# Attention plus linear attention on one core: normalisation in pieces, a new start, two spare PSUM banks in the first chunk, a reordered tail

## Chip, cores, metric

One core of one Trainium2 chip. The metric is the device time of one execution in microseconds (us). Times are medians of several executions. The engines are TensorE (PE in the profile, PEld for its weight loads), VectorE (DVE), ScalarE (ACT), GpSimd (POOL) and SyncE (SP).

## The reference, cut to what matters

```python
# B, S, D = 1, 2048, 640; 32 heads of 20; all bf16
q, k, v = split_heads(x @ wqkv)                    # part A
p = softmax(einsum("bhqd,bhkd->bhqk", q, k) * 20 ** -0.5)
a = merge_heads(einsum("bhqk,bhkd->bhqd", p, v)) @ wo

pq, pk = phi(q), phi(k)                            # part B, its own x, wqkv, wo
num = einsum("bhqd,bhde->bhqe", pq, einsum("bhsd,bhse->bhde", pk, v))
b = merge_heads(num / (pq . sum(pk) + 1e-6)) @ wo  # linear attention
out = concatenate([a, b], axis=-1)
```

Part A needs 2048 x 2048 x 32 exponentials. They fix the time: everything else has to fit beside them.

## The kernel before

A *unit* is one head's scores for 128 keys and 512 queries, one PSUM bank. There are 2048 units. They are handled in groups of three: TensorE writes the scores of a group in three banks, ScalarE takes one exp over the three, TensorE multiplies the result with V ("PV"). Two sets of three banks alternate, one bank collects PV, and one *spare bank* serves all other matmuls: the Q, K and V projections, the output projection and all of part B. These run in the background, in steps that fill the spare bank and are copied out by VectorE. One *chunk* is 64 units: a group of 4 heads against 512 queries. At its end the PV result is normalised.

The main loop, in program order. In the timelines shown below, each engine works through its own instructions in this order:

```python
for j in range(NG):                     # NG groups
    if j + 1 < NG:
        self.emit_scores(j + 1)         # TensorE
    self.emit_exp(j)                    # ScalarE
    self.flush_later(j)                 # what self.at(dj, ...) put off to this group
    ...                                 # emit_pv, and norm(n) at the end of a chunk
    ...                                 # budget: 1600 columns while j < 30, later less
    self.bg(budget)                     # background steps into the spare bank
    self.ahead(min(j + 4, NG - 1))
    self.fill(1200 if j > 20 else 0)    # idle matmuls that keep TensorE busy
```

The normalisation: five VectorE instructions, straight one behind the other.

```python
sch.op("dve", lambda e: e.tensor_copy(self.OTr[:, sl], ps[:, b, sl]), ...)
sch.op("dve", lambda e: e.transpose(tr, self.OTr[:, sl]), ...)
sch.op("dve", lambda e: e.reciprocal(rt, tr[:, 0:w:32]), ...)
sch.op("dve", lambda e: e.transpose(tr, rt.unsqueeze(2).broadcast_to(...)), ...)
sch.op("dve", lambda e: e.tensor_tensor(self.OTn[:, os_, sl], tr, self.OTr[:, sl], op=ALU.mult), ...)
```

The end of a Q or K projection step, which frees the spare bank:

```python
sch.op("dve", lambda e: e.tensor_copy(dst, ps[:, b, :]), reads=(("ps", b),), writes=(res,))
sch.op("dve", lambda e: e.tensor_reduce(mx, dst, axis=AX.X, op=ALU.max, ...), ...)
```

The loads: SyncE issues the rows of x and then 15 transposed loads of x (three sets of five, one set for each further 512 tokens). At the same time ScalarE's queue brings three weight loads of 800 KB.

## Time and profile before

1056.07 us, median of 3 runs (1055.41 to 1056.4). The profiled execution took 1050.0 us with a span of 1048.2, so it is one of the quicker ones.

From the page: busy times; the chain that ended last, by engine and by line; and the two costliest groups of instructions (after "|" the busy time and the mean ns of one, then the engine's idle time before them and what ended it).

```profile
PE 791.8 (76%) x5849; PEld 256.7 (24%) x5905; DVE 381.4 (36%) x752; ACT 952.7 (91%) x743; POOL 26.9 (3%) x42
...
ACT 65%; PE 21%; DVE 11%; issue 1%; DMA 1%; SPq 0%; POOL 0%; POOLq 0%; DVEq 0%
...
L1045 ACT ACTIVATE f_PT<-ps 128x1536 bf16<-128x1536 f32 (+1 forms) x683 | 935.5, 1551 | 67.7 <-PE ps L153 67.0
L153 PE MATMUL ps<-f_Qr,f_KT 32*128 32x512 bf16 x2048 | 285.9, 413 | 159.8 <-ACT f_PT L1045 151.3
```

ScalarE is the bound. The exps fill 935.5 us, and when ScalarE waits for one, it waits for scores. The question is only when it idles. I cut the span in four: to the first exp; from there to the end of unit 72; from there to the end of the last exp; the tail. The windows view gives busy time by engine for the last three (columns: length, PE, PEld, DVE, ACT, POOL, granted clock, DMA share, GB/s). ScalarE's idle time is the length less its busy time. Where the timeline merges exps into one entry, the end of unit 72 is interpolated in it.

```profile
11.61:51.59 39.98, 32.88 (x255) 13.47 (x258) 17.27 (x31) 33.03 (x25) 22.57 (x31) 0.91 0.64 103
51.59:1033.58 981.99, 747.30 (x5525) 237.09 (x5576) 349.54 (x692) 915.59 (x712) 1.10 (x4) 0.90 0.05 14
1033.58:1048.20 14.62, 5.87 (x37) 2.92 (x35) 7.45 (x18) 1.59 (x4) 0.00 (x0) 0.81 0.14 49
```

So 6.9 us idle in the first part, 66.4 us in the middle, and a tail of 14.62 us. The middle is where the time is. The timeline around the end of the fourth chunk shows one of its stalls (columns: start, length, what; in brackets the idle time before it and what ended it):

```profile
146.84 0.69 DVE L1079 COPY f_OTr<-ps 128x512 f32<-128x512 f32 x1 [2.04 <-PE ps L153]
147.42 0.39 PE L153 MATMUL ps<-f_Qr,f_KT 32*128 32x512 bf16 x3 [0.63 <-ACT f_PT L1045]
147.57 0.71 DVE L1086 STREAM_TRANSPOSE f_Tr<-f_OTr 128x512 f32<-128x512 f32 x1
148.31 0.25 DVE L1087 RECIPROCAL f_Rt<-f_Tr 128x16 f32<-128x16 f32 x1
148.60 0.71 DVE L1088 STREAM_TRANSPOSE f_Tr<-f_Rt 128x512 f32<-128x512 f32 x1
149.35 0.69 DVE L1091 TENSOR_TENSOR f_OTn<-f_Tr,f_OTr 128x512 bf16<-128x512 f32 x1
149.96 0.68 DVE L983 CAST f_KT<-ps 128x512 bf16<-128x512 f32 x1
150.68 0.69 DVE L984 TENSOR_REDUCE f_kmx<-f_KT 128x1 f32<-128x512 bf16 x1
151.10 1.49 PE L153 MATMUL ps<-f_xT,f_arw 128*128 128x512 bf16 x3 [3.29 <-DVE f_KT L983]
152.52 0.61 PE L153 MATMUL ps<-f_Qr,f_KT 32*128 32x512 bf16 x3
...
153.18 1.45 ACT L1045 ACTIVATE f_PT<-ps 128x1536 bf16<-128x1536 f32 x1 [3.13 <-PE ps L153]
```

Read it from the bottom. The exp at 153.18 waited 3.13 us for scores. TensorE could not issue them, because ahead of them in its order stood a K projection that waited 3.29 us for the spare bank. The copy that frees the bank (the CAST at 149.96) stood behind the five instructions of the normalisation. The projection matmuls that follow take 1.49 us for three: TensorE had also lost half of its clock (0.50 granted from 150 to 158 us).

### The profile page before, as it was taken

The numbers are of one execution on the slowest core, as the hardware profiler recorded it, in microseconds if no ns is written. First come the engines' busy times: TensorE is split into PE (matmuls) and PEld (weight loads), VectorE is DVE, ScalarE is ACT, GpSimd is POOL, SyncE is SP. The second block draws the span as 40 slices with busy tenths as digits, with TensorE's granted clock in tenths as the row PEclk, the third lists the DMA queues.
The fourth block names the chain that finished last, engine by engine and source line by source line (L and its number), as shares of the span: only waits on it lengthen the run. The fifth ranks groups of instructions, "written<-read, shape, count | busy, mean of one in ns | idle before, by whom it ended". The sixth has DMA issues, their size and how long they took to land.

```text
span 1048.2 us, 13498 instructions
## 1 busy us (share of the span) xinstructions
PE 791.8 (76%) x5849; PEld 256.7 (24%) x5905; DVE 381.4 (36%) x752; ACT 952.7 (91%) x743; POOL 26.9 (3%) x42
## 2 busy tenths in 40 slices
PE   6888778877787786777777777877777877768775
PEld 3332322322222222222221212212212222112222
DVE  4544344434323334333222443244341243352123
ACT  4979889999899999999998989888999989998895
POOL 5400000000000000000000000000000000000000
PEclk8989989999889989899998878878999889997898
DMA  8400000050001010010001000100000000000000
GB/s 197 62 1 1 1 1 1 1 151 1 8 13 32 1 26 1 2 26 1 1 13 38 2 0 14 38 1 7 25 21 13 13 7 14 7 1 14 13 1 28
DMA packets 40410, 20.81 MB, mean 20 GB/s; under 512 B 31896, under 2 KB 39704, under 8 KB 40344
## 3 DMA queue, kind: packets, MB, share of 16 engines
q1 hardware_dynamic: 37064, 17.21, 7.0%
q10 hardware_dynamic: 3280, 2.66, 0.9%
q8 instruction: 48, 0.79, 0.3%
q14 instruction: 18, 0.15, 0.0%
HBM read 7.41 MB, written 5.24 MB: 12 GB/s over the span
## 4 chain that ended last, share of the span: by engine, by line
ACT 65%; PE 21%; DVE 11%; issue 1%; DMA 1%; SPq 0%; POOL 0%; POOLq 0%; DVEq 0%
ACT f_PT L1045 63%; PE ps L153 21%; DVE f_Tr L1088 2%; DVE f_Tr L1086 2%; DVE f_OTr L1079 2%; ACT f_ex L1207 2%; DVE f_OTn L1091 2%; DMA f_xT<-in_A_x_dram 1%; DVE f_KT L983 1%; DVE f_Rt L1087 1%; DVE f_r L1204 0%; SPq L889 0%; DVE f_pk L1345 0%; PE ps L1357 0%; DVE f_Qr L983 0%
## 5 line engine op out<-in xcount | busy, mean ns | idle before, releaser
L1045 ACT ACTIVATE f_PT<-ps 128x1536 bf16<-128x1536 f32 (+1 forms) x683 | 935.5, 1551 | 67.7 <-PE ps L153 67.0
L153 PE MATMUL ps<-f_Qr,f_KT 32*128 32x512 bf16 x2048 | 285.9, 413 | 159.8 <-ACT f_PT L1045 151.3
L153 PE MATMUL ps<-f_PT,f_V 128*21 128x512 bf16 x2048 | 217.1, 419 | 0.0
L153 PEld LDWEIGHTS ps<-f_Qr,f_KT 32*128 32x128 bf16 x2048 | 66.8, 92 | 385.1 <-ACT f_PT L1045 324.7
L153 PEld LDWEIGHTS ps<-f_PT,f_V 128*21 128x21 bf16 x2048 | 49.7, 89 | 130.1 <-issue 128.7
L153 PE MATMUL ps<-f_arw,f_arb 128*128 128x320 bf16 x320 | 66.4, 320 | 11.5 <-DVE f_r L1204 11.2
L153 PE MATMUL ps<-f_wo,f_OTn 128*128 128x320 bf16 x256 | 59.8, 339 | 14.7 <-DVE f_OTn L1091 6.0
L1204 DVE COPY f_r<-ps 128x320 f32<-128x320 f32 (+1 forms) x52 | 29.5, 566 | 92.6 <-PE ps L153 92.6
L983 DVE CAST f_Qr<-ps 128x512 bf16<-128x512 f32 x32 | 22.1, 690 | 86.5 <-PE ps L153 86.5
L153 PE MATMUL ps<-f_xT,f_arw 128*128 128x512 bf16 x144 | 43.8, 404 | 11.6 <-DVE f_KT L983 4.9
L153 PE MATMUL ps<-f_xT,f_wqp 128*128 128x512 bf16 x134 | 45.5, 411 | 5.4 <-issue 4.0
L153 PE MATMUL ps<-f_woB,f_pk 128*128 128x320 bf16 x160 | 37.7, 359 | 14.5 <-DVE f_st L1386 6.4
L1079 DVE COPY f_OTr<-ps 128x512 f32<-128x512 f32 (+1 forms) x33 | 22.2, 674 | 68.9 <-PE ps L153 68.8
L1210 DVE TENSOR_SCALAR f_ex<-f_ex 128x320 f32<-128x320 f32 (+1 forms) x52 | 18.9, 364 | 70.5 <-ACT f_ex L1207 70.5
L1173 DVE CAST f_st<-ps 128x320 bf16<-128x320 f32 x24 | 11.8, 490 | 83.6 <-PE ps L153 83.6
L1207 ACT ACTIVATE f_ex<-f_r 128x320 f32<-128x320 f32 (+1 forms) x52 | 32.3, 621 | 9.7 <-DVE f_r L1204 9.7
L983 DVE CAST f_KT<-ps 128x512 bf16<-128x512 f32 x32 | 22.1, 689 | 47.0 <-PE ps L153 47.0
L153 PE MATMUL ps<-f_arw,f_xT 128*128 128x160 bf16 x320 | 32.3, 250 | 8.8 <-DVE f_KT L983 7.5
L1386 DVE CAST f_st<-ps 128x320 bf16<-128x320 f32 x32 | 15.7, 490 | 60.4 <-PE ps L153 60.4
L153 PE MATMUL ps<-f_arb,f_arw 128*128 128x512 bf16 x90 | 32.2, 427 | 6.6 <-DVE f_r L1204 4.7
L153 PEld LDWEIGHTS ps<-f_arw,f_arb 128*128 128x128 bf16 x320 | 26.1, 101 | 45.2 <-issue 21.1
L153 PEld LDWEIGHTS ps<-f_wo,f_OTn 128*128 128x128 bf16 x256 | 19.9, 104 | 46.9 <-issue 21.0
(73 smaller groups left out, 426.4 us busy)
## 6 DMA issues: line engine op xcount, KB each, us to landing
out_dram<-f_st SPq DMA_DIRECT2D x32, 160.0 KB, 1.8
f_arw<-in_B_wqkv_dram SPq DMA_DIRECT2D x1, 2400.0 KB, 8.4
f_arb<-in_A_wqkv_dram ACTq DMA_DIRECT2D x2, 800.0 KB, 12.0
f_arw<-in_A_wqkv_dram ACTq DMA_DIRECT2D x1, 800.0 KB, 8.8
f_wo<-in_A_wo_dram SPq DMA_DIRECT2D x4, 200.0 KB
f_woB<-in_B_wo_dram SPq DMA_DIRECT2D x1, 800.0 KB, 10.1
f_st<-in_A_x_dram SPq DMA_DIRECT2D x2, 320.0 KB
f_arb<-in_B_x_dram SPq DMA_TRANSPOSE x40, 2.7
```

Of the source, the lines that this page charges most:

```text
L153: lambda e: e.matmul(out, lhsT, rhs, start=start, stop=stop, tile_position=tp, skip_group_check=sgc),
L983: sch.op("dve", lambda e: e.tensor_copy(dst, ps[:, b, :]), reads=(("ps", b),), writes=(res,))
L1045: sch.op("act", lambda e: e.activation(self.PT[:, s0:s0 + n, :], ps[:, b0:b0 + n, :], AF.Exp, scale=scale), reads=tuple(("ps", b0 + k) for ...
L1079: sch.op("dve", lambda e: e.tensor_copy(self.OTr[:, sl], ps[:, b, sl]), reads=(("ps", b),), writes=(("OTr", k),))
L1086: sch.op("dve", lambda e: e.transpose(tr, self.OTr[:, sl]), reads=res, writes=(("Tr", k),))
L1088: sch.op("dve", lambda e: e.transpose(tr, rt.unsqueeze(2).broadcast_to([128, w // 32, 32])), reads=(("Rt", k),), writes=(("Tr", k),))
L1091: sch.op("dve", lambda e: e.tensor_tensor(self.OTn[:, os_, sl], tr, self.OTr[:, sl], op=ALU.mult), reads=(("Tr", k),) + res, writes=wr)
L1173: sch.op("dve", lambda e: e.tensor_copy(dst, ps[:, b, 0:320]), reads=(("ps", b),), writes=(("stage", s, h),))
L1204: sch.op("dve", lambda e: e.tensor_copy(tt, ps[:, b, 0:n]), reads=(("ps", b),), writes=(("r1", k),))
L1207: sch.op("act", lambda e: e.activation(ex, tt, AF.Exp), reads=(("r1", k),), writes=(("ex", k),))
L1210: sch.op("dve", lambda e: e.tensor_scalar(ex, ex, 1.0, 1e-6, op0=ALU.min, op1=ALU.add), reads=(("ex", k),), writes=(("ex", k),))
L1386: sch.op("dve", lambda e: e.tensor_copy(dst, ps[:, b, 0:320]), reads=(("ps", b),), writes=(("stage", s, h),))
```

## The change

Its intent: (1) give the normalisation out in pieces over the next three groups, and put off the max-reductions, the mask steps and phi's exp; (2) start sooner: a warm-up of TensorE, the first Q and K tiles in pieces on two engines, and the weight loads after the first set of transposed loads, through GpSimd's queue; (3) in the first 72 units groups of 3, 2, 3, 2, 3, 2, 2, 1, which free a second spare bank; (4) output partials done before the last exp, and a tail without stores between the halves. The core of the diff:

```diff
-            sch.op("dve", lambda e: e.transpose(tr, self.OTr[:, sl]), ...)
-            sch.op("dve", lambda e: e.reciprocal(rt, tr[:, 0:w:32]), ...)
-            ...
+            def f1(...): ...      # transpose
+            def f2(...): ...      # reciprocal
+            def f3(...): ...      # transpose
+            def f4(...): ...      # multiply, then norm_done(n)
             if last:
-                self.tail_out(range(4 * qc + 2 * k, 4 * qc + 2 * k + 2))
+                for f in (f1, f2, f3, f4):
+                    f()
+            else:
+                for d, f in ((1, f1), (2, f2), (2, f3), (3, f4)):
+                    self.at(d, f)
+        if last:
+            self.tail_out(range(4 * qc, 4 * qc + 4))
... (step_qk)
-            sch.op("dve", lambda e: e.tensor_reduce(mx, dst, ...), ...)
+            self.at(2, lambda: sch.op("dve", lambda e: e.tensor_reduce(mx, dst, ...), ...))
... (consts: 8 zero matmuls; Q copied by ScalarE, K by VectorE in 128 and 384 columns)
+        for k, off in ((0, D_MODEL), (1, 0)):
+            sch.dma("pool", lambda e, k=k, off=off: e.dma_start(self.wst[k], ...),
+                    reads=(("xT", N_DC - 1, 1),), writes=(("wst", k),))
+        sch.dma("pool", lambda e: e.dma_start(self.wv[:, :, 160:D_MODEL], ...), ...)
... (run)
-        self.groups = [list(range(u, min(u + 3, nunits))) for u in range(0, nunits, 3)]
+            w = (3, 2, 3, 2, 3, 2, 2, 1)[len(self.groups) % 8] if u < 72 else 3
-        self.AUX = (7,)
+        self.AUX = (7, 5)                  # (7,) again from unit 72 on
+                if j > NG - 28:
+                    budget = 1200
... (one step per spare bank and group, not one per group; mask steps at groups 44 to 52;
     phi's exp two groups later; credit capped at 1.3 budgets, not 2; ahead() looks 2 or 3 groups ahead in the first ten)
```

## The prediction

> **What bounds the kernel now.** ScalarE: the page has ACT busy 952.7 of 1048.2 us, and the chain that ended last is 63% exps. By groups of instructions, 682 exps over three banks cost 934.5 us; undisturbed (timeline), 38 take 51.32 us, 1.35 us each. What can be won is ACT's 95 us of idle time. By stage windows:
>
> - Before the first exp (11.61 us): 9 us.
> - To 66 us: 14 us. 4.07 us wait for a transposed load landing at 16.85, behind 2.4 MB of weights; 7 us follow the first normalisation (52 to 66), where mask steps add to it.
> - 66 to 1034 us: 60 us, nearly all in the 12 us behind the normalisations (60.4 us with the first). Timeline: copy, transpose, reciprocal, transpose, multiply hold VectorE 3.1 us in one block; the next Q/K copy queues behind it, the one spare PSUM bank stays full, TensorE (in order) stops, the next exp's scores are late: about 2 us each. The pause also drops the granted clock: 0.50 at 54 to 62 us, 512-column matmuls at 0.43 us, not 0.22. The Trainium skill, "TensorE: Matmul & The Clock Gate", "The HAM clock gate", says the array halves its clock after an idle window of about 3.4 us and needs as much sustained work to recover[...].
> - Last exp to end: 14.6 us. Output partials still need the spare bank, so the last PV is 2.7 us late; then two normalisation halves with stores of the first between.
>
> **What the change does.**
> 1. Normalisation in pieces over three groups, each at most 1 us; mask, max-reductions and phi's exp moved later: a copy waits 1 us, not 3.1, and TensorE stays warm. 60 us idle become about 12: -48.
> 2. Start: weights after the first transposed loads, eight zero matmuls as warm-up, Q evacuated by ACT (0.6 us) beside K in two pieces on VectorE: first exp at about 9.3 us: -2.3.
> 3. First chunk: groups of 3,2,3,2,3,2,2,1 free bank 5, so projections overlap their copies. 72 units take 32 exps, not 24. Two banks take 1.20 us against 1.55 alone, so about 1.0 us back to back, one bank 0.62 (estimates from those durations): +2 us. With the 4.07 us wait mostly gone and the 52-to-66 stall cut: -7 net.
> 4. Tail: the instruction order puts all partials before the last exp, no first-half copies on VectorE between the halves: -4.5.
>
> Sum -62; I take 4 back for new waits: **998 us**, 8 in 10 within **984 to 1016**. Faster by over 2%: 0.97; within 2%: 0.025; slower: 0.005.
>
> **What would show it.** (1) ACT idle from 66 us to the last exp 8 to 20 us, no waits of 2 to 3 us behind a normalisation, granted clock from 0.905 to 0.93 or more. (2) First exp at 8.5 to 10 us; no wait of 4 us near 16 to 20. (3) Unit 72 done near 46 us, not 51.6. (4) Last exp to end 9 to 11 us. ACT busy about 950.
>
> **What would make it wrong.** If the stalls come from the single spare bank or the low clock itself, not from the 3.1 us block, half the 60 us stays: about 1025. If the weights, now sent by the Pool queue after the transposes, come too late for group 1, or TensorE limits the first chunk (1600 columns of background per smaller group), it gains nothing.

## The result, and the profile after

994.15 us, median of 4 runs (993.58 to 1000.69), against 1056.24 in the same rounds. The ratio is 0.9426, 95% interval 0.9386 to 0.9466. Ratios in this document are the mean time of one kernel's runs over that of the other's of the same rounds, so not quite the ratio of the medians quoted. All outputs are right.

The page of the profiled execution, which is the slowest of the four (span 997.0, 1000.69 us):

```profile
PE 788.6 (79%) x5905; PEld 249.8 (25%) x5905; DVE 370.1 (37%) x751; ACT 951.5 (95%) x754; POOL 27.3 (3%) x44
...
ACT 79%; PE 14%; DVE 3%; DMA 2%; SPq 1%; issue 0%; DVEq 0%
...
L1092 ACT ACTIVATE f_PT<-ps 128x1536 bf16<-128x1536 f32 (+1 forms) x691 | 938.2, 1648 | 32.9 <-PE ps L162 31.5
```

ScalarE does the same work in a shorter span, and VectorE is nearly gone from the chain (11% to 3%). The same three stretches:

```profile
9.04:60.81 51.77, 42.33 (x315) 18.00 (x316) 23.95 (x44) 35.26 (x32) 26.84 (x39) 0.90 0.59 99
60.81:987.27 926.46, 734.65 (x5519) 225.93 (x5516) 338.63 (x686) 910.96 (x711) 0.00 (x0) 0.94 0.05 14
987.27:997.00 9.73, 4.10 (x26) 2.19 (x26) 4.69 (x12) 2.18 (x7) 0.00 (x0) 0.91 0.21 73
```

The middle idles 15.5 us where it idled 66.4. The tail lost 4.9 us. But the first part is 11.8 us *longer* than before, 51.77 for 39.98. The same normalisation as above, now:

```profile
143.13 14.22 ACT L1092 ACTIVATE f_PT<-ps 128x1536 bf16<-128x1536 f32 x10
...
146.09 0.69 DVE L1126 COPY f_OTr<-ps 128x512 f32<-128x512 f32 x1 [1.41 <-PE ps L162]
...
147.30 0.70 DVE L1136 STREAM_TRANSPOSE f_Tr<-f_OTr 128x512 f32<-128x512 f32 x1
148.01 0.39 PE L162 MATMUL ps<-f_Qr,f_KT 32*128 32x512 bf16 x3 [0.35 <-ACT f_PT L1092]
148.03 0.25 DVE L1139 RECIPROCAL f_Rt<-f_Tr 128x16 f32<-128x16 f32 x1
148.32 0.71 DVE L1142 STREAM_TRANSPOSE f_Tr<-f_Rt 128x512 f32<-128x512 f32 x1
148.33 0.61 PE L162 MATMUL ps<-f_PT,f_V 128*21 128x512 bf16 x8
148.95 0.65 DVE L1026 CAST f_KT<-ps 128x512 bf16<-128x512 f32 x1
149.35 0.39 PE L162 MATMUL ps<-f_Qr,f_KT 32*128 32x512 bf16 x3 [0.41 <-ACT f_PT L1092]
149.53 0.67 DVE L1146 TENSOR_TENSOR f_OTn<-f_Tr,f_OTr 128x512 bf16<-128x512 f32 x1
149.68 0.82 PE L162 MATMUL ps<-f_xT,f_arw 128*128 128x512 bf16 x3
```

The copy of K now stands between two pieces. The scores wait only for the exp before them (0.35 and 0.41 us, "ACT f_PT"), which is how it should be when ScalarE is the bound. Ten exps run through this stretch without a gap (the first line).

And what went wrong in the first part:

```profile
18.28 0.60 ACT L1092 ACTIVATE f_PT<-ps 128x512 bf16<-128x512 f32 x1 [0.36 <-PE ps L162]
...
27.15 1.04 PE L162 MATMUL ps<-f_xT,f_arw 128*128 128x512 bf16 x2 [8.58 <-DMA f_xT<-in_A_x_dram]
...
28.77 1.45 ACT L1092 ACTIVATE f_PT<-ps 128x1536 bf16<-128x1536 f32 x1 [9.89 <-PE ps L162]
```

TensorE waits 8.58 us for the second set of transposed loads, and ScalarE 9.89 us behind it. This wait was not there before. In two further profiles of the same kernel it is 5.64 and 4.44 us; its size varies, and the profiled execution above is the unlucky one.

### The profile page after: what moved, and what is told of

It reads as the page before. It is cut to its first block, busy times and chain, and to the rows that moved or that the text cites. A ratio compares the mean times of both kernels' runs of the same rounds, so it can differ in the third digit from the quotient of the medians.

```text
span 997.0 us, 13565 instructions
## 1 busy us (share of the span) xinstructions
PE 788.6 (79%) x5905; PEld 249.8 (25%) x5905; DVE 370.1 (37%) x751; ACT 951.5 (95%) x754; POOL 27.3 (3%) x44
## 3 DMA queue, kind: packets, MB, share of 16 engines
q0 software_dynamic: 496, 2.25, 1.1%
## 4 chain that ended last, share of the span: by engine, by line
ACT 79%; PE 14%; DVE 3%; DMA 2%; SPq 1%; issue 0%; DVEq 0%
ACT f_PT L1092 77%; PE ps L162 14%; ACT f_ex L1271 2%; DMA f_xT<-in_A_x_dram 2%; SPq L902 1%; DVE f_OTr L1126 0%; DVE f_xT L1230 0%; DVE f_xT L1232 0%; DVE f_Tr L1136 0%; DVE f_arb L1276 0%; DVE f_pk L1411 0%; DVE f_Tr L1142 0%; DVE f_ex L1274 0%; DVE f_OTn L1146 0%; PE ps L1423 0%
## 5 line engine op out<-in xcount | busy, mean ns | idle before, releaser
L162 PE MATMUL ps<-f_PT,f_V 128*21 128x512 bf16 x2048 | 212.4, 409 | 1.3 <-ACT f_PT L1092 0.7
L162 PE MATMUL ps<-f_arw,f_arb 128*128 128x320 bf16 x320 | 69.7, 322 | 2.1 <-DVE f_va L1316 1.5
L162 PE MATMUL ps<-f_wo,f_OTn 128*128 128x320 bf16 x256 | 54.6, 322 | 6.2 <-DVE f_xT L1232 4.2
L162 PE MATMUL ps<-f_xT,f_arw 128*128 128x512 bf16 (+2 forms) x165 | 45.8, 379 | 9.0 <-DMA f_xT<-in_A_x_dram 8.6
L162 PE MATMUL ps<-f_xT,f_wqp 128*128 128x512 bf16 x160 | 49.1, 384 | 1.6 <-DVE f_pk L1411 0.8
L162 PE MATMUL ps<-f_arb,f_arw 128*128 128x512 bf16 x100 | 35.9, 443 | 2.1 <-DVE f_r L1268 1.0
L1271 ACT ACTIVATE f_ex<-f_r 128x320 f32<-128x320 f32 (+1 forms) x52 | 37.1, 713 | 0.0
L1316 DVE CAST f_va<-ps 128x320 bf16<-128x320 f32 x32 | 15.7, 490 | 57.0 <-PE ps L162 57.0
L162 PE MATMUL ps<-f_woB,f_pk 128*128 128x320 bf16 x160 | 32.7, 307 | 2.3 <-DVE f_pk L1411 1.9
```

The costliest lines, as they stand in the source:

```text
L162: lambda e: e.matmul(out, lhsT, rhs, start=start, stop=stop, tile_position=tp, skip_group_check=sgc),
L1271: sch.op("act", lambda e: e.activation(ex, tt, AF.Exp), reads=(("r1", k),), writes=(("ex", k),))
L1316: sch.op("dve", lambda e: e.tensor_copy(dst, src), reads=(("ps", b), "va1"), writes=(("va", tl, h),))
```

## The experiments

All stage numbers (us) in one place, each from one profiled execution; "idle" is ScalarE's:

| kernel | first exp | unit 72 done | idle between | last exp ends | idle in the middle | tail | median time |
|---|---|---|---|---|---|---|---|
| before | 11.61 | 51.6 | 6.9 | 1033.6 | 66.4 | 14.6 | 1056.1 |
| changed (first profile) | 9.04 | 60.8 | 16.5 | 987.3 | 15.5 | 9.7 | 994.2 |
| changed (e1_after) | 9.48 | 56.1 | 11.3 | 982.2 | 15.1 | 9.6 | 994.4 |
| changed (e7_after) | 9.57 | 55.7 | 10.8 | 979.8 | 12.9 | 9.8 | 993.7 |
| e2_late3 | 9.52 | 59.2 | 14.4 | 985.6 | 15.2 | 9.6 | 996.5 |
| e3_split | 9.99 | 50.7 | 5.5 | 977.3 | 15.6 | 9.8 | 989.0 |
| e4_early | 10.43 | 53.0 | 7.4 | 976.6 | 12.8 | 11.9 | 990.4 |
| e5_b_norm | 12.04 | 51.2 | 6.3 | 978.2 | 16.7 | 16.9 | 993.5 |
| e6_a_block | 9.06 | 58.9 | 14.5 | 1045.4 | 70.1 | 10.4 | 1061.1 |
| e8_nodefer | 9.43 | 57.0 | 12.4 | 982.3 | 13.9 | 9.6 | 995.4 |
| e9_onebank | 8.90 | 46.3 | 4.8 | 962.6 | 6.6 | 9.6 | 975.4 |
| e10_tail | 9.46 | 57.4 | 12.7 | 983.7 | 14.8 | 22.0 | 1001.4 |
| e11_paced | 9.20 | 51.0 | 7.7 | 969.8 | 9.5 | 9.6 | 982.9 |
| e12_best | 9.70 | 43.1 | 0.9 | 957.4 | 5.4 | 9.8 | 972.7 |

Two tails need a note. In e4_early the last copy comes 6.1 us after the last exp, as in the changed kernel; what makes its tail longer is a late semaphore record of ScalarE. And the profile of e10_tail is that of its slowest run (1007.37 us).

The changed kernel was run twice more as a base on the same chip: e1_after with the three load experiments, e7_after with e8 to e10.

> The changed kernel as it is, for a base on the same chip as the next three. Both theories: 994 us (ratio to before 0.941), and again a ScalarE wait of 8 to 10 us near 19 to 29 us that ends with the landing of the transposed loads of tokens 1024 to 1535.

> The changed kernel again, as a base for the next three on the same chip: 994 us.

Measured: 994.42 us, ratio to before 0.9427, and 993.68 us, ratio 0.9431. The wait near 19 us came back smaller than I wrote, 5.6 us.

### Is it the block of normalisation?

**e5_b_norm**: the kernel before with part (1)'s pieces and nothing else.

```diff
-            (transpose, reciprocal, transpose, multiply at once)
+            if last: (at once, as before)
+            else:
+                for d, f in ((1, f1), (2, f2), (2, f3), (3, f4)):
+                    self.at(d, f)
```

> The kernel before, with only the normalisation given out in pieces over three groups (one spare bank, groups of three, loads, start, tail, the other postponed steps all as before). Theory N (the 3.1 us block on VectorE in front of the next bank copy is the stall): ScalarE idle between 66 us and the last exp falls from 60 to 15 to 25 us, time 1010 to 1022, granted clock up to 0.93 or more. Rival S (one spare bank or the low clock is the cause, and the new budget and postponed reductions are needed): idle stays over 40 us, time 1035 or more.

Measured: 993.52 us (990.62 to 996.87), ratio to before 0.9418 (0.9369 to 0.9466). The idle time of the middle fell from 66.4 to 16.7 us, as theory N had it; the time is some 20 us better than I had reckoned. The pieces alone give as much as the *whole* change: 0.9418 here, 0.9426 to 0.9431 for the changed kernel. All its other parts together come to nothing, as a sum: below, one of them turns out to cost 18 us, which is about what the rest bring.

**e6_a_block**: the changed kernel with the block back.

```diff
-            if last:
+            if True:
                 for f in (f1, f2, f3, f4):
                     f()
```

> The changed kernel with the normalisation back in one block, all else kept. Theory N: ScalarE idle in the middle back to 45 to 60 us, time 1024 to 1040. Rival S: idle stays under 30 us, time 1000 to 1010.

Measured: 1061.08 us, ratio to before 1.0078 (1.0024 to 1.0132): the whole gain is gone, and the time is within 2% of before. Theory N named the direction; both numbers are above its ranges (1024 to 1040 us, 45 to 60 us idle). The middle stretch of e5_b_norm, then that of e6_a_block:

```profile
51.23:978.16 926.93, 724.44 (x5521) 233.33 (x5570) 342.95 (x691) 910.21 (x712) 1.10 (x4) 0.94 0.05 14
```

```profile
58.87:1045.42 986.55, 756.28 (x5469) 231.49 (x5513) 343.32 (x684) 916.47 (x711) 0.00 (x0) 0.89 0.05 13
```

Read the length less ACT: 16.7 against 70.1 us idle. VectorE is busy 343 us in both, so no work was saved; only its order differs. The granted clock falls with the stalls (0.94 to 0.89). ScalarE is busy 6 us more in the second, because an exp after a gap takes 1.45 us and one without a gap 1.35. Of rival S, the single spare bank has fallen as a cause: e5_b_norm keeps it. The clock is not separated, since it moves with the block: how much of each 3 us wait is the block and how much the half clock behind it (1.49 us for three matmuls instead of 0.82), no run here shows.

**e8_nodefer**: the changed kernel with the other postponed steps put back.

```diff
-            self.at(2, lambda: sch.op("dve", ... tensor_reduce ...))
+            sch.op("dve", ... tensor_reduce ...)
-            self.at(20 + 2 * c, cmp)
+            cmp()
-        self.at(2, act); self.at(3, fin)
+        self.at(1, act); self.at(2, fin)
```

> The changed kernel with the other postponed steps put back: the max-reductions straight behind their copies, the five mask steps in one go, the exp of phi one group later and not two. If these share in the gain of the middle: 999 to 1006. If the pieces of the normalisation are all of it: 993 to 997.

Measured: 995.35 us, ratio to before 0.9444, against 0.9431 for the changed kernel of the same rounds. The intervals overlap widely. The other postponements do nothing that these rounds can show.

### The wait near 19 us

Theory A: the weight loads, released the moment the first set of transposed loads has landed (11.07 us), share the DMA engines with the second set. The three loads bring 2.25 MB.

**e2_late3**: they wait for the last set.

```diff
-                    reads=(("xT", N_DC - 1, 1),), writes=(("wst", k),))
+                    reads=(("xT", N_DC - 1, 3),), writes=(("wst", k),))
```

> The changed kernel, with the two big weight loads held back until the last of the fifteen transposed loads has landed, not the fifth. Theory A (the 9.9 us wait is the 2.2 MB of weights sharing the DMA engines with the transposed loads): the wait at 19 us falls under 2 us, the third set of transposed loads lands by 20 us; but the weights of group 1 come about 10 us later, so a new wait of 3 to 7 us for them near 30 us; time 988 to 993. Theory B (the transposed loads are slow by themselves, or held by the issuing queue): the wait at 19 us stays 8 to 10 us, time 994 or more.

Measured: 996.54 us, ratio 0.945 against 0.9427 for e1_after. The wait at 19 us is gone (0.49 us in its place), and the slowest transposed load takes 5.7 us from issue to landing, where it was 15.0 in the first profile and 11.1 in e1_after. The new wait for the weights of group 1 is 6.76 us and so a little longer than what it replaced:

```profile
19.84 7.43 ACT L1092 ACTIVATE f_PT<-ps 128x1536 bf16<-128x1536 f32 x6 [0.49 <-PE ps L162]
34.03 1.02 ACT L1092 ACTIVATE f_PT<-ps 128x1024 bf16<-128x1024 f32 x1 [6.76 <-PE ps L162]
```

Theory A holds for the cause; the time missed my range by 3.5 us.

**e3_split**: as e2_late3, and the 80 columns of Q and of K that group 1 needs loaded by themselves at the start.

```diff
+        for k, off in ((0, D_MODEL), (1, 0)):
+            sch.dma("act", lambda e, k=k, off=off: e.dma_start(self.wst1[:, k],
+                    awq[:, :, off + 80:off + 160]), writes=(("wst1", k),))
```

> As the kernel that holds the weights back, and the columns of group 1 loaded apart at the start (0.2 MB). Theory A: neither wait is left, first chunk 8 to 11 us shorter, time 982 to 987. Theory B: 993 to 996.

Measured: 988.96 us, ratio 0.9377, that is 5.3 us better than e1_after of the same rounds (0.0050 of 1055). Both waits are gone. No run of one overlaps with the other (985.5 to 990.4, 991.8 to 995.5). It is 2 us short of my range, because I had reckoned with the 9.9 us of the first profile and the usual wait is about 5.

**e4_early**: all weight loads at the start on ScalarE's queue, as before the change.

```diff
+        sch.dma("act", ... wv[:, :, 160:640]); sch.dma("act", ... wst[0]); sch.dma("act", ... wst[1])
-        (the three loads on GpSimd's queue, waiting for the first set of transposed loads)
```

> The changed kernel, with all weight loads issued at the start by the ScalarE queue, as in the kernel before. Theory A: the loads are over before the third set of transposed loads, so the wait of 9.9 us at 19 us goes, and the 4 us wait near 16 us of before comes back, first exp within 1 us of 9.04: time 987 to 992, so that moving the loads was a loss of 2 to 7 us. Theory C (moving the loads was right, and all else would be worse): first exp later than 10.5 us and time 996 or more.

Measured: 990.37 us, ratio 0.9401, about 3 us better than e1_after (0.0026 of 1055 is 2.7 us; the means of the six runs differ by 3.1). The first exp is 1.0 us later than in e1_after (10.43, so my "within 1 us of 9.04" missed), the wait near 16 us is 1.39 us and not 4. The first exp is later because ScalarE now issues the loads itself: its table load starts at 5.84 us, not 2.44. Moving the loads was a small loss in sum. With this margin the intervals of e4_early and e1_after still overlap; the stage table (53.0 against 56.1) points the same way.

Why a later, shorter burst hurts more than an earlier one is argued, not shown. The DMA queues to 45 us of the changed kernel, then to 30 us of the kernel before (packets, MB, share of 16 engines; q1 holds the transposed loads, q0 and q10 the weights):

```profile
q1 hardware_dynamic: 8704, 2.62, 32.2%
q0 software_dynamic: 496, 2.25, 25.2%
```

```profile
q1 hardware_dynamic: 8704, 2.62, 47.5%
q10 hardware_dynamic: 3280, 2.66, 32.1%
```

A transposed-load packet has 300 bytes (2.62 MB over 8704), a packet of GpSimd's queue 4.5 KB on average, one of ScalarE's queue 0.8 KB. The Trainium skill, "DMA: Bandwidth & Descriptors", "Queues, rings and completion order", says each DMA engine takes its queues in turn "at *packet* granularity". If a packet of the profile is a packet in that sense, which no run here shows, each small packet waits behind 4.5 KB instead of 0.8 KB. But the landings do not bear this out: the slowest transposed load took 11.0 us in the kernel before and 10.1 us in e4_early, beside the small packets, and 10.4 to 15.0 us in the changed kernel, beside the large ones. It may matter more which set of loads is in flight, and when its data are asked for. The cause stays open; no run here changed the packet size alone.

### Two spare banks

**e9_onebank**: the changed kernel with groups of three and one spare bank from the start.

```diff
-            w = (3, 2, 3, 2, 3, 2, 2, 1)[len(self.groups) % 8] if u < 72 else 3
+            w = 3
-        self.AUX = (7, 5)
+        self.AUX = (7,)
```

> The changed kernel with groups of three throughout and one spare bank from the start: 24 exps for the first 72 units, not 32. If the second bank earns its price: the exps cost 2 us less but new waits behind bank copies cost 5 to 10, time 997 to 1002. If the price eats it up: 992 to 995.

Measured: 975.36 us, ratio to before 0.9259 against 0.9431: 18 us *faster* than the changed kernel. Both of my expectations were wrong, so I needed another theory. The first stretch of e7_after, then that of e9_onebank:

```profile
9.57:55.68 46.11, 41.07 (x310) 17.96 (x316) 23.95 (x44) 35.27 (x32) 26.84 (x39) 0.96 0.55 111
```

```profile
8.90:46.33 37.43, 31.76 (x250) 13.05 (x255) 16.75 (x30) 32.61 (x25) 26.84 (x39) 0.91 0.65 124
```

ScalarE is busy 2.7 us less with 24 exps than with 32, and it idles 4.8 instead of 10.8 us. TensorE is about as busy in both, 89% of the stretch with two banks and 85% with one, but with two it does more before unit 72 is through. Counting columns in the order of instructions, TensorE has 56,064 background columns in front of the scores of unit 72 with two banks, and 38,400 with one (7,680 of both lie before the first scores). The 17,664 more are 7.4 us at 0.215 us for 512 columns (an estimate from the undisturbed matmuls of this trace). The reason is in the program: each group, however small, gets the budget of 1600 columns and now one step *per bank*. So whatever the second bank gained by overlapping copies, it let more background work in where TensorE had no room. That work is not urgent, and later stretches have room for it.

A rival lies in the loads. In e7_after ScalarE waits 4.44 us behind the second set of transposed loads; in e9_onebank no matmul waits for a transposed load, though the slowest takes 10.9 us there too, and after 20.76 us ScalarE runs without a gap:

```profile
20.76 40.46 ACT L1092 ACTIVATE f_PT<-ps 128x1536 bf16<-128x1536 f32 x30 [1.43 <-PE ps L162]
```

So the early wait takes both the released loads and the two banks. It does not explain all of the difference: e3_split and e12_best (below) have no such wait, with two banks and with one, and their first stretches still differ by 7.2 us (40.7 and 33.4), 2.7 us of it busy time. And the first stretch is only half of the 18 us: from e7_after to e9_onebank it shrinks by 8.7 us, the middle by 7.8.

**e11_paced** tests the budget: small groups and two banks as in the change, but the budget in proportion to the group.

```diff
-            self.bg(budget)
+            self.bg(budget * len(self.groups[j]) / 3 if j < self.n2 else budget)
```

> The changed kernel with its small groups and its two spare banks, but in that stretch the background budget is scaled by the size of the group (two thirds for a group of two), so that by unit 72 TensorE has 44,544 background columns behind it, not 56,064 (one bank and groups of three: 38,400). Theory O (the first chunk is lost because more background columns per unit are put on a TensorE that is the limit there; 11,520 columns fewer are 4.8 us at 512 columns in 0.215 us): time 980 to 987, the rest of the distance to 975 being the dearer exps and the early DMA wait. Rival G (the small groups and the second bank themselves cost it, whatever the budget): 991 to 995.

Measured: 982.86 us, ratio 0.9316: inside the range of theory O, 12 us better than the changed kernel (0.9431, of other rounds and another chip), out of the 18 that e9_onebank gave. Rival G's range is missed. The first stretch got 4.3 us shorter (41.8 for 46.1) for 11,520 columns fewer, where 4.8 us were expected; so the budget is shown as half of the 8.7 us that this stretch had to give. The other half stays with the small groups and the second bank: 1.5 us of busy time and 2.9 us of idle time, with a wait of 4.05 us behind the transposed loads still there. One thing stays open: e9_onebank and e11_paced also idle less in the middle (6.6 and 9.5 us against 12.9), which is after the stretch that the edit touches. Most of this lies far behind it, between units 1024 and 1536 (5.7 us in e7_after, 1.1 and 1.2 in the other two). The later background steps fall at other places; I did not test which of them collide. That the time fell into the range of theory O is in this part luck.

### The tail

**e10_tail**: the tail of before.

```diff
-        if last: self.tail_out(range(4 * qc, 4 * qc + 4))      # after both halves
+                self.tail_out(...)                             # after each half
-                if tl < 2 or h == 0:                           # ScalarE copies 6 of 8
+                if h == 0:                                     # 4 of 8
-                if j > NG - 28:
-                    budget = 1200
```

> The changed kernel with the tail of before: no raised budget for the output partials, stores of the first normalisation half between the halves and half of the copies on VectorE. Last exp to end back from 9.7 to 13 to 15 us; time 997 to 1000. If the work only moves into the exps before, ScalarE waits of 0.2 us there go (about 2 us in all) and the time is 995 to 997.

Measured: 1001.41 us, ratio 0.9501 against 0.9431, 7 us more. The tail of the profiled run takes 22.0 us, more than the 14.6 of before, so my range for it was too low; this is the slowest run, and 12 us more tail than in e7_after cannot be that of the median one. The timeline after the last exp (983.65 us) shows output partials still in work, at half clock (seven matmuls in 2.05 us, where the kernel before took 1.12 us for seven):

```profile
984.34 2.05 PE L162 MATMUL ps<-f_wo,f_OTn 128*128 128x320 bf16 x7 [0.57 <-DVE f_xT L1230]
...
987.50 2.05 PE L162 MATMUL ps<-f_wo,f_OTn 128*128 128x320 bf16 x7 [1.11 <-DVE f_xT L1230]
...
990.66 2.05 PE L162 MATMUL ps<-f_wo,f_OTn 128*128 128x320 bf16 x7 [1.11 <-DVE f_xT L1230]
...
992.64 0.61 PE L162 MATMUL ps<-f_PT,f_V 128*21 128x512 bf16 x4
```

The last PV (992.64) comes 9 us after the exp it needs, because three partials stand before it in TensorE's order. In pieces, the normalisation ends three groups later. I take it that the partials therefore start later and that the raised budget at the end makes up for it; this run puts three things back at once, so which of them does it is not shown. e5_b_norm, which has the pieces and not the new tail, fits: its tail is 16.9 us, 2.3 longer than before.

### All together

**e12_best**: one bank and groups of three (e9_onebank), group 1's weights apart (e3_split), and the ones of V set by GpSimd at the start.

```diff
-        sch.op("dve", lambda e: e.memset(self.V[:, :, :, 0:1], 1.0), writes=("Vones",))
+        sch.op("pool", lambda e: e.memset(self.V[:, :, :, 0:1], 1.0), writes=("Vones",))
```

> Three lessons together: the changed kernel with groups of three and one spare bank from the start, the weight columns of group 1 loaded apart and the big loads after all transposed loads, and the ones of V set by GpSimd at the start instead of by VectorE near 11 us. The waits of 2.9, 0.5 and 1.4 us before 21 us in the one-bank kernel go by half or more, so 970 to 974 against 975.4. If the early wait is something else, 974 to 977.

Measured: 972.72 us (969.02 to 974.95), ratio to before 0.9227 (0.9201 to 0.9253): the best kernel here, 83 us under before and 21 under the change. Between the first exp and the end of unit 72 ScalarE idles 0.9 us. From 17.56 us it runs at least 62 exps in one go, to 101 us, with one spare bank (the last line):

```profile
9.70:43.13 33.43, 29.86 (x255) 12.35 (x255) 16.40 (x29) 32.50 (x25) 15.34 (x26) 1.00 0.41 107
43.13:957.42 914.29, 720.30 (x5575) 227.98 (x5575) 346.33 (x700) 908.87 (x712) 9.35 (x9) 0.97 0.07 16
...
17.56 83.45 ACT L1102 ACTIVATE f_PT<-ps 128x1536 bf16<-128x1536 f32 x62 [0.43 <-PE ps L162]
```

## Why the prediction was right, and where a step of it failed

The time was predicted as 998 with 984 to 1016, and is 994. The main mechanism was right, and one step was wrong in sign. The middle gave more than was written and the reserve for new waits was not needed, and this made up for it: that the sum came out so close is in part luck.

- **"A copy waits 1 us, not 3.1 ... 60 us idle become about 12: -48."** Right, and now shown by itself both ways: the pieces alone take the middle from 66.4 to 16.7 us idle (e5_b_norm), the block alone takes the middle of the changed kernel back to 70.1 (e6_a_block). In the changed kernel the middle idles 12.9 to 15.5 us in its three profiles. Granted clock 0.936 to 0.950 for 0.905, as foretold; but the pauses are not all that lowers it (see the last section).
- **"I take 4 back for new waits."** Not needed in the middle; there it went the other way. The exps got some 4.5 us quicker (ACT busy 915.6 us before, 911.0 and 911.2 after), because fewer of them follow a gap. That term was not in my sum.
- **"First exp at about 9.3 us: -2.3."** Right: 9.04 to 9.57. The warm-up does what it should: 18 transposes of 128 columns take 1.18 us after it, 2.10 us before the change. The Trainium skill, "TensorE: Matmul & The Clock Gate", "The HAM clock gate", asks for about 3.4 us of sustained work; the eight zero matmuls run for 3.59 us. No run leaves the warm-up out, so its share of the 2 us is not shown; e4_early gives about 1 us to the loads that ScalarE no longer issues at the start.
- **"The 4.07 us wait mostly gone ... -7 net", unit 72 "near 46 us".** Wrong, and this is the step that failed. Unit 72 was done at 55.7 to 60.8 us, later than the 51.6 of before. Two things stood in place of the gain. First, a new wait of 4.4 to 9.9 us for the second set of transposed loads, which I had not looked at: I had asked when the *first* set would land and not what the released loads would collide with (e2_late3 and e3_split show the cause; e9_onebank shows that with one bank the same loads are not waited for). Second, the small groups with two banks overloaded TensorE: 17,664 background columns more, about 7 us by the estimate, against the gain that I had written for bank 5 (e11_paced took 11,520 of them away and got 4.3 us back). My text had named this as what would make it wrong, "TensorE limits the first chunk", and still booked it as a gain. The price of the small exps was about right, +2 predicted, 2.7 measured. The Trainium skill, "ScalarE: Activation LUTs", "What ACT_TABLE_LOAD costs", would have been a better source for it than the single 1.20 us exp that I took: its 186 ns + 0.833 ns per column gives 612, 1039 and 1466 ns for 512, 1024 and 1536 columns, and the trace has 0.60, 1.02 and 1.45 us for lone exps.
- **"Tail ... -4.5."** Right: 9.6 to 9.8 for 14.6 us. That the pieces themselves would have lengthened the tail by 2.3 us (e5_b_norm) I had not seen.

In stages, with e7_after: start -2.0, first stretch +6.1, middle -57.9, tail -4.8, together -58.6 us of span. My sum in the same stages was -2.3; -3.3 (unit 72 at 46 instead of 51.6, less the start); about -52 (the -48, and what is then left of the -7); -4.5; and +4 in reserve: together -58. The first stretch missed by 9 us; the middle, with its quicker exps and without new waits, gave 6 us more, and the reserve of 4 was not needed. That the errors cancel is luck.

## What to carry to other kernels

When an engine executes strictly in order, look at what stands *in front of* the short instruction that frees a shared buffer: cutting a 3.1 us block in pieces gained 61 us here, with nearly the same busy time on VectorE. More buffers are no gain where they only let in more background work ahead of what the bounding engine waits for; budget background work by the time that the bounding engine gives, not by the step of a loop. A load moved out of one transfer's way lands in that of the next: follow it to the transfers that are in flight when it starts.

## What the Trainium skill lacked or had wrong

- "Perfetto Trace Analysis", "Optimizing Tensor Performance", "Matmuls", advises to rotate independent matmul groups through different banks so that the copy of one overlaps the matmuls of the next. It does not say that this can cost: here a second bank in the first 72 units, bought with smaller exps and with an unscaled budget, made the kernel 18 us slower (993.7 against 975.4), and with one bank e12_best runs 62 exps without a gap.
- No page gives a number for what a block of VectorE instructions in front of a bank copy costs the other engines. Here 3.1 us of it cost about 2 us per chunk (61 us over 32 chunks), and the granted clock of the whole run was 0.905 with the block and 0.937 with the pieces.
- "DMA: Bandwidth & Descriptors", "Queues, rings and completion order", gives the turn-taking by packet, and no number for what it does to transposed loads. Here the slowest of them took 10 to 15 us from issue to landing beside the weights, in packets of 0.8 KB as of 4.5 KB, and 5.7 us without.
- "TensorE: Matmul & The Clock Gate", "The HAM clock gate", ties the half clock to an idle window of about 3.4 us, and the prediction followed it. Here windows that were half busy were enough; a later section of the page names frequent short pauses, without a figure. In the changed kernel the clock fell with ScalarE busy throughout and matmuls in 1.96 of 3.41 us (the windows before and after the fall):

```profile
295.45:298.86 3.41, 1.96 (x19) 0.60 (x19) 0.49 (x1) 3.41 (x4) 0.00 (x0) 1.00 0.13 48
298.86:302.27 3.41, 3.41 (x20) 0.87 (x16) 0.00 (x0) 3.41 (x3) 0.00 (x0) 0.50 0.02 5
```

  In all, 24 falls of the changed kernel's clock came after 3.41 us with 0 to 2.30 us of matmuls, and none after more; windows that no fall followed had 2.10 us or more (counted over the clock and matmul records of this trace). In front of the fall that the prediction spoke of, at 52.88 us in the kernel before, matmuls ran for 1.37 of 3.41 us. So stretches without a stall lost clock too, which is part of why the changed kernel stays at 0.94.
